# Two modulation weight loads on ScalarE's queue, filler matmuls of 512 columns and a new table of issue in a one-core block of conditioned layer norms, dilated local attention and a token-mixing MLP

## The chip, the core and the metric

The kernel runs on one NeuronCore of a Trainium2 chip. The core has five engines, each with an instruction queue of its own that it works through in order: TensorE (PE in the profile; its weight loads are listed apart as PEld), VectorE (DVE), ScalarE (ACT), GpSimd (POOL) and SyncE (SP), which here only issues DMAs. Sixteen DMA engines move data. The metric is the device time of one execution in microseconds (us); shorter is better.

## What is computed

The input x has 2048 tokens of 512 features. A vector c of 512 numbers gives six modulation vectors; the block normalises, attends and mixes over tokens. Cut to what matters:

```python
mod = (silu(c) @ w_mod).reshape(1, 6, 1, 512)
sa, ca, ga, sb, cb, gb = (mod[:, i] for i in range(6))
h = layernorm(x) * (1 + ca) + sa
x = x + ga * A(h)          # attention
h = layernorm(x) * (1 + cb) + sb
x = x + gb * B(h)          # MLP over tokens

def A(x):                  # 32 heads of 16; 8 keys per query, 2 tokens apart
    q, k, v = split(x @ wqkv)
    idx = pos[:, None] - 2 * arange(8)      # masked where negative
    attn = softmax(q . k[idx] / 4)
    return (attn . v[idx]) @ wo

def B(x):                  # mixes over the 2048 tokens, hidden size 1792
    h = layernorm(x)
    u = gelu(einsum('sd,sf->df', h, w1) + b1)
    return (einsum('df,fs->ds', u, w2) + b2).T
```

All inputs are bfloat16. The parts of w_mod are numbered 0 to 5 in the order sa, ca, ga, sb, cb, gb.

## The kernel before

**Operations and order.** The kernel does not emit instructions where its loops stand. Each step is added to a graph (`add`, `G.add_any`) with a name, the engines it may run on, what it reads and writes and the buffers it takes and frees. `G.schedule` (lines 87 to 114) then walks through `ORDER` (lines 180 to 232), a table of names written out ahead, and every engine gets its instructions in that order. A suffix picks the engine: `:a` ScalarE, `:d` VectorE, `:p` GpSimd, `:s` nothing where the step may be skipped. `:q` on a TensorE step makes `mm` (line 512) issue each matmul as four of 32 output columns; I call these narrow, the others full. Since every engine works in order, an instruction that waits holds up everything behind it in its queue.

**Stages.** The 16 tiles of 128 tokens are worked in five chunks of 2, 4, 4, 4 and 2 tiles.

- *Loads:* `ld_x*` bring x (128 KB a tile; x0 and x1 singly, the others in pairs: `ld_x_1_2` is the pair of tiles 2 and 3 of chunk 1), `ld_wqkv0` to `2` the three parts of wqkv and `ld_wmod0` to `5` the six of w_mod (512 KB each). All are issued by SP through `dma` (line 352); ScalarE issues `ld_c` and later some of the stores.
- *Modulation:* TensorE turns c into columns (`cps`), ScalarE and VectorE make SiLU of it (`silu_exp`, `silu_dve`), and TensorE multiplies it with parts 1 and 0 of w_mod: `modcols1` gives 1 + ca (`a1col`), `modcols0` gives sa (`sab`, from which `qvb0` and `qvb1` make biases of q and v). Parts 2 to 5 give rows (`modrow`, `mrows`, `ld_row*`), one of which scales the output weights (`woq_s`).
- *Filler:* `warm0` is a group of matmuls of the identity with itself, issued behind `cps` while TensorE has nothing to do; `warm1` and up can be placed anywhere or skipped (lines 518 to 528, 533).
- *First norm:* `ln1s*` (statistics, on VectorE, or on ScalarE as two passes with `ln1v*` behind them), `rstd1_*` and `nb1_*`, `n1_*` (the normalised tile). Chunks 0 and 1 are transposed by TensorE (`tr*`) and copied with the scale 1 + ca (`hT*`), chunks 2 to 4 by DMA (`xt*`), and `wsc*` scales the weights for them.
- *Attention of a chunk:* `qkv{chunk}_{t}{j}` are four column groups each of q, k and v (t = 0, 1, 2), copied out by `ev*`. VectorE multiplies q with the eight shifted k (`qk{chunk}_{0..3}`), TensorE adds up over a head (`red*`), then the softmax (`max`, `sub`, `exp`, `esum`, `rcp`, `smB`). SP copies the weights (`a2_*`) and v (`vd*`) to other partitions; VectorE multiplies them (`pv*`), TensorE adds up (`pvacc*`), `oev*` copies out.
- *Output and second norms:* `wo*` is the output projection of a tile. With `x1_*` on ScalarE it has a fifth matmul that adds the residual; with `:d` VectorE adds it. Then `ln2q`, `ln2m`, `n2_*`, the modulation `aff*` of a whole chunk on VectorE, `ln3s`, `nb3_*` and the normalised input `h3_*` of the MLP. `halo_v*` copies the last values of v into the next chunk's buffer.
- *MLP:* `mlp1_{part}_{f}_{tile}` accumulates hidden group f over tokens as far as h3 is there; `park` and `padd` store and add partial sums, `gelu`, then `mlp2_*`, `fin*` and the stores `st_out*`.

**DMA semaphores.** DMAs take turns at eight semaphores, over both queues together, and one that takes a semaphore waits until the DMA that had it before has landed.

All instructions stand in the profile under line 131, the helper that records them, so tiles and operations tell them apart. The lines that the change touches:

Of the kernel before, what the change touches and what calls it, by code (L numbers as in the profile page):

```python
# [185 lines left out]
rstd1_2 nb1_2 n1_7:p ev0_00 ln1s10 n1_9 ln1s11 ev0_10 ld_x_4_14 warm2:s n1_6 qkv1_10 n1_8 qk0_1 qk0_0 qkv0_12 ev0_12  # L186
qk0_2 qk0_3 ln1v11 qkv1_00 ld_wmod4 ln1v10 qkv0_22 ln1v12 qvb1 ld_wmod2 ev1_00 ln1v13 rstd1_3 nb1_3 qkv0_20 qvb_cp1
red0_0 ev1_10 wsc2_3 red0_1 ln1s14:a red0_2 red0_3 mask ld_wo0 xt6 ev0_20 ev0_22 ln1v14 ld_wmod5 vd0_1 qkv1_01 max0
qk1_0 ev1_03 sub0 qkv1_13 wsc1_2:p exp0 ev1_13 qk1_3 xt8 esum0 qkv1_11 halo_v1:a qkv1_02:q ev1_01 rcp0 smB0 ev1_11
wsc0_2:a qkv1_12 qkv1_20 wsc2_2:a wsc0_0:a ev1_02 qk1_1 xt9 xt7 qkv1_22 ev1_12 a2_0_1 wsc1_0:a wsc1_1:a a2_0_2 a2_0_0  # L190
qkv2_00 n1_11:p a2_0_3 ev1_20 qkv1_23:q red1_0 red1_1 qkv1_21:q wsc2_1:a qk1_2 pv0_1 vd0_0 ln1s15:a red1_2 red1_3
ev2_00 pv0_0 ev1_23 vd0_3 n1_10 qkv2_11:q ev1_21 n1_13 max1 pvacc0_0 ln1v15 qkv2_12 vd0_2 pv0_3 ev2_12 ld_wmod3 ld_wo1
qkv2_10 sub1 ev2_10 pvacc0_1 ev1_22 xt10 qkv2_02 exp1 ld_wo3 modrow pv0_2 ev2_02 mrows vd1_2 qkv2_01:q ld_wo2 pvacc0_2
qkv2_13 ev2_11 vd1_3 ld_row0 esum1 qkv2_03 qk2_0 xt11 wsc2_0:a qk2_2 pvacc0_3 ev2_01 vd1_1 qk2_1 qkv2_22:q ev2_13 rcp1
rstd1_4 oev0_2 xt13 ev2_03 oev0_0 smB1 qk2_3 qkv2_20 halo_v2:a woq_s a2_1_2 nb1_4 red2_0 n1_12 red2_1 red2_2 ev2_20
ev2_22 a2_1_3 qkv2_21 red2_3 a2_1_1 qkv2_23:q n1_15 ev2_21 wo0 x1_0 a2_1_0 ev2_23 wo1:q max2 xt12 vd1_0 pv1_2 ln2q0
x1_1 ln2q1 ld_row1 sub2 exp2 qkv3_03:q pvacc1_2 n1_14:p qkv3_22 ld_b2 ev3_22 pv1_3 ln2m0 ev3_03 qkv3_13 vd2_2 esum2
rstd2_0 qkv3_00 qkv3_02 pv1_0 nb2_0 qkv3_01 rcp2 pv1_1 xt14 oev1_2 ev3_00 smB2 vd2_3 ld_row2 n2_1 pvacc1_0 ev3_13
a2_2_2 a2_2_3 n2_0 ev3_01 ev3_02 xt15 qk3_3 qkv3_12:q pvacc1_1 qkv3_10 qkv3_11 oev1_1 ev3_10 oev1_0 pvacc1_3 ev3_12
aff0 qkv3_21 oev1_3 wo2:q a2_2_0 ev3_11 ln3s0:a qk3_0 wo5 wo3 ln3s1:a ln3v0 x1_5 x1_2 halo_v3:a wo4 x1_3 qkv4_00  # L200
a2_2_1 qk3_1 qk3_2 x1_4 ln2q3 red3_0 vd2_1 red3_1 pv2_3 qkv3_20 ln2q2 ln2q5 ev3_21 ln2q4 ld_b1 qkv4_10:q biascols
ev3_20 qkv4_12:q red3_2 ln2m2 rstd2_2 pv2_1 ev4_10 nb2_2 ev4_00 red3_3 pvacc2_3 max3 ev4_12 qkv4_20:q qkv4_22 sub3
qkv4_02:q n2_2 qkv3_23 n2_5 oev2_3 ld_w1_0_0 ln3v1 n2_4 rstd3_0 exp3 pv2_2 pvacc2_2 ld_w1_0_896 ev4_02 vd2_0
ld_w1_0_512 n2_3:p ev3_23 oev2_2 pvacc2_1 pv2_0 nb3_0 oev2_1 aff2 pvacc2_0 esum3:q oev2_0 wo9 rcp3 biascols_cp vd3_2
smB3 ev4_20 vd3_3 wo7 h3_1:p ln3s5 ln3s4 ln3v4 ln3s3:a h3_0:p wo6 wo8 ln3v5 x1_7 x1_9 ln3v3 ln3s2 halo_v4:a x1_6
mlp1_0_0_0 ln3v2 mlp1_0_3_0 rstd3_2 mlp1_0_2_0 qk4_0 x1_8 nb3_2 h3_4:d red4_0 vd3_0 ld_w2_4 h3_5 h3_2:d mlp1_0_8_0
warm1:s warm3:s h3_3 mlp1_0_1_0 ln2q7 mlp1_0_0_2:q a2_3_3 qk4_1 ln2q6 ln2q9 vd3_1 red4_1 a2_3_1 mlp1_0_2_2:q ln2q8
qk4_2 mlp1_0_1_2:q park0_0 park0_1 red4_2 qk4_3 red4_3 a2_3_2 a2_3_0 mlp1_0_3_2 ln2m6 rstd2_6 pv3_1 ld_w1_0_1152 nb2_6
max4 ev4_22 mlp1_0_5_0 park0_2 mlp1_0_4_0 n2_9 mlp1_0_4_2 mlp1_0_6_0 sub4 pv3_0 mlp1_0_5_2 n2_7 n2_6 mlp1_0_8_2 vd4_0
mlp1_0_6_2 pv3_3 park0_3 park0_4 ld_w2_0 pvacc3_0 park0_5 exp4 oev3_0 park0_6 ld_row3 pvacc3_1 mlp1_0_7_0:q pvacc3_3  # L210
mlp1_0_7_2:q pv3_2 esum4:q mlp1_0_10_0:q oev3_1 n2_8 ld_w1_0_1408 rcp4 aff6 pvacc3_2 smB4 oev3_3 mlp1_0_10_2 oev3_2
ln3s6:a a2_4_2 wo12 ln3s9 ln3s7:a ln3v9 x1_12:d wo13 x1_13:d ln2q12 ln3s8 ln3v8 wo11 ln3v7 ln3v6 mlp1_0_12_0
mlp1_0_12_2 wo10 x1_11:d a2_4_0 rstd3_6 nb3_6 a2_4_1 vd4_2 a2_4_3 mlp1_0_9_0 h3_8:d mlp1_0_9_2 x1_10:d ln2q13 h3_9
h3_7:d vd4_1 ln2q10 pv4_2 vd4_3 ln2q11 ln2m10 rstd2_10 mlp1_0_11_0 pv4_3 nb2_10 h3_6:p mlp1_0_7_6 mlp1_0_8_6 pv4_0
mlp1_0_9_6 pv4_1 park0_7 ld_w2_1 park0_8 mlp1_0_11_2 n2_11 n2_12 n2_13 n2_10:d aff10 ln3s13 park0_9 mlp1_0_10_6 ln3v13
pvacc4_2 pvacc4_3 oev4_2 mlp1_0_12_6:q ld_w1_0_1664 ld_w2_2 pvacc4_0 pvacc4_1 oev4_0 mlp1_0_11_6 wo15 x1_15:d
ld_w1_1_0 big_done wo14 x1_14:d ln3s11 mlp1_0_13_0 mlp1_0_13_2 ld_w1_1_640 park0_10 park0_11 park0_12 ln2q15 ln2q14
ln2m14 mlp1_0_13_6 rstd2_14 mlp1_1_1_6 ln3s12 nb2_14 n2_14 mlp1_1_0_6 ln3s10 n2_15:p ln3v12 aff14 mlp1_1_4_6 ln3v11
ln3v10 warm5:s rstd3_10 nb3_10 h3_10 h3_13:p ln3s14 ln3v14 mlp1_1_5_6 ln3s15 ln3v15 mlp1_1_6_6 mlp1_1_0_10 mlp1_1_4_10
h3_12:p park0_13 mlp1_1_2_6 rstd3_14 ld_w1_1_896 mlp1_1_1_10 mlp1_1_6_10 nb3_14:s h3_11 mlp1_1_2_10 padd1_0 h3_14:d  # L220
ld_w2_7 h3_15:d padd1_1 mlp1_1_5_10 mlp1_1_3_6 mlp1_1_3_10 padd1_2 padd1_3 padd1_4 mlp1_1_10_10 padd1_10 mlp1_1_7_10
padd1_7 mlp1_1_8_10 gelu7 gelu10 mlp1_1_9_10 ld_w1_2_0 padd1_5 padd1_6 mlp1_2_0_11 mlp1_2_4_11 mlp1_2_0_14 padd1_9
gelu9 mlp1_2_1_11 ld_w1_1_1408 padd2_0 padd1_8 gelu0 mlp1_2_3_11 mlp1_2_3_14 mlp1_2_1_14 padd2_1 mlp1_2_2_11
ld_w1_2_640 mlp1_2_5_11 mlp1_2_5_14 padd2_3 gelu1 mlp1_2_2_14 padd2_5 gelu5 mlp1_1_11_10 ld_w2_5 padd2_2 gelu3
mlp1_2_4_14 padd2_4 ld_w2_15 padd1_11 gelu2 gelu4 mlp1_2_6_11 mlp1_1_13_10 gelu8 gelu11 ld_w2_9 padd2_6 mlp1_1_12_10
# [798 lines left out]
```

## Time and profile before

| | us |
|---|---|
| median of 3 runs | 202.74 |
| lowest, highest | 201.93, 203.73 |
| the profiled execution | 201.83 |
| its span in the profile | 199.6 |
| granted TensorE clock over it | 1.00 |

The profile is of one execution. PE, PEld, DVE, ACT and POOL are the busy times of the engines; a "q" behind an engine's name is its queue of DMA issues and waits. A line of the order of time gives the start, the length, the engine, the operation, out<-in by tile names and a count; in brackets stands the idle time ahead of it and what ended it. q1 is SP's DMA queue and q10 is ScalarE's. Where I give the start or landing of one step, it is read from the trace by the step's place in its engine's order.

### The profile page before, as it was taken

What the parts mean: (1) busy time and instruction counts of PE and PEld (TensorE: products, weight loads), DVE (VectorE), ACT (ScalarE), POOL (GpSimd) and SP (SyncE); (2) the same over time, 40 slices, a digit from 0 to 9 for tenths busy, and PEclk for the clock granted to TensorE, in tenths of its full rate; (3) what the DMA queues carried; (4) which work ended last, traced back from release to release, by engine and by line L of the source; (5) the groups of instructions that cost most, each with busy time, mean ns of one, the idle gap of its engine ahead of it and who ended that gap; (6) DMA issues with size and microseconds to landing.
All of it is one profiled execution on the core that took longest, in us unless ns stands there. A gap on an engine that the chain in (4) does not pass through costs nothing.

```text
span 199.6 us, 4192 instructions
## 1 busy us (share of the span) xinstructions
PE 189.8 (95%) x1652; PEld 96.2 (48%) x1652; DVE 157.2 (79%) x229; ACT 125.9 (63%) x285; POOL 17.7 (9%) x41
## 2 busy tenths in 40 slices
...
GB/s 152 339 365 319 62 220 174 205 268 189 181 276 50 184 347 132 113 298 168 193 246 20 241 221 200 305 213 243 211 193 168 122 22 155 113 79 26 79 54 55
DMA packets 55367, 35.92 MB, mean 180 GB/s; under 512 B 24628, under 2 KB 52788, under 8 KB 55348
## 3 DMA queue, kind: packets, MB, share of 16 engines
...
q10 hardware_dynamic: 1592, 1.38, 2.1%
...
q14 instruction: 6, 0.05, 0.1%
...
## 4 chain that ended last, share of the span: by engine, by line
PE 40%; DVE 29%; ACT 12%; DMA 8%; SPq 6%; issue 3%; ACTq 0%; DVEq 0%
PE psS L131 39%; DVE big L131 18%; DVE h L131 7%; SPq L131 6%; ACT junk L131 4%; DMA wst<-in_A_wqkv_dram 4%; ACT h L131 3%; DMA out_dram<-h 2%; DMA hT<-h 2%; ACT xx L131 1%; DMA a2sb<-lsb 1%; PE psL L131 1%; DVE st L131 1%; DVE xx L131 1%; DVE m L131 1%
## 5 line engine op out<-in xcount | busy, mean ns | idle before, releaser
L131 PE MATMUL psS<-h,wst 128*128 128x512 bf16 (+1 forms) x296 | 51.2, 379 | 0.4 <-ACT h L131 0.4
L131 PEld LDWEIGHTS <-wst 128*128 128x128 bf16 (+1 forms) x458 | 34.8, 101 | 34.3 <-issue 4.1
L131 DVE TENSOR_TENSOR big<-a2sb,vD 128x4096 bf16<-128x4096 bf16 (+1 forms) x20 | 36.6, 1860 | 1.8 <-PE psL L131 0.8
L131 DVE TENSOR_TENSOR big<-q_sb,k_f 128x4096 bf16<-128x4096 bf16 (+1 forms) x20 | 36.4, 1858 | 0.1
L131 PE MATMUL psS<-hT,w_qkv 128*32 128x256 bf16 (+3 forms) x312 | 30.3, 332 | 1.0 <-DMA hT<-h 1.0
L131 DVE SCALAR_TENSOR_TENSOR h<-psS,bcol,rows_bc 128x512 f32<-128x512 f32 (+2 forms) x18 | 12.4, 690 | 21.0 <-PE psS L131 20.7
L131 PEld LDWEIGHTS <-w_qkv 128*32 128x32 bf16 (+1 forms) x354 | 19.0, 109 | 18.4 <-issue 4.8
L131 PE MATMUL psS<-gT,big 128*128 128x512 bf16 x112 | 24.8, 379 | 0.0
L131 ACT ACTIVATE junk<-xx 128x512 bf16<-128x512 bf16 x28 | 17.6, 627 | 2.6 <-DVE xx L131 1.4
L131 PEld LDWEIGHTS <-big 128*128 128x128 bf16 x144 | 11.9, 97 | 14.9 <-DMA big<-in_w_mod_dram 1.6
L131 ACT ACTIVATE h<-xx,nb,rs 128x512 bf16<-128x512 bf16 x21 | 16.4, 809 | 2.4 <-DVE nb L131 2.3
L131 PE MATMUL psS<-woq,o_sb 128*128 128x512 bf16 (+1 forms) x88 | 16.0, 380 | 0.3 <-ACT o_sb L131 0.3
L131 ACT ACTIVATE gT<-psS,bcol 128x512 bf16<-128x512 f32 x14 | 8.9, 686 | 9.9 <-DVE psS L131 9.9
L131 DVE TENSOR_TENSOR psS<-psS,gT 128x512 f32<-128x512 f32 x14 | 9.2, 696 | 6.3 <-PE psS L131 6.2
L131 DVE TENSOR_TENSOR h<-h,xx 128x512 bf16<-128x512 f32 (+2 forms) x18 | 11.4, 633 | 3.4 <-DMA out_dram<-h 2.7
L131 POOL TENSOR_SCALAR h<-xx,rs,nb 128x512 bf16<-128x512 bf16 x8 | 6.3, 790 | 76.6 <-DVE nb L131 45.5
L131 PEld LDWEIGHTS <-group 128*32 128x32 bf16 x288 | 6.5, 95 | 11.4 <-issue 4.6
L131 PE MATMUL psS<-hT,wst 128*128 128x256 bf16 (+2 forms) x76 | 11.5, 337 | 0.0
L131 ACT ACTIVATE v_sb<-psS,qvb 128x512 bf16<-128x512 f32 (+1 forms) x20 | 11.3, 597 | 0.0
L131 DVE TENSOR_TENSOR h<-h,rows_bc 128x2048 bf16<-128x2048 bf16 (+1 forms) x10 | 10.6, 1055 | 0.8 <-ACT gT L131 0.5
L131 PE MATMUL psS<-big,group 128*32 128x512 bf16 (+1 forms) x160 | 10.0, 339 | 0.8 <-ACT q_sb L131 0.6
L131 ACT ACTIVATE q_sb<-psS,qvb 128x512 bf16<-128x512 f32 (+1 forms) x18 | 10.6, 614 | 0.1
...
## 6 DMA issues: line engine op xcount, KB each, us to landing
...
```

Of the source, the lines that this page charges most:

```text
L131: r = fn(*a, **k)
```

## The change

Three things change. `dma` gets a parameter for the issuing queue, and `ld_wmod1` and `ld_wmod0` are issued by ScalarE. The filler matmuls read the 128 columns of the identity four times over, so each has 512 columns, and their counts are 12 for `warm0` and 2 for the others (64 and 16 of 128 columns before). And the whole table of issue is new; in it only `warm7` and `warm0` are not skipped (`warm0` alone before).

```diff
-    WARM=(64, 16, 16, 16, 16, 16),
+    WARM=(12, 2, 2, 2, 2, 2, 2, 2),
...
-    def dma(out_ap, in_ap, nbytes, reads, writes, name, rate=350e3, issue=0.5, lat=2.0, row=1024, **kw):
-        return add("sp", issue, lambda: nc.sync.dma_start(*(a() if callable(a) else a for a in (out_ap, in_ap))),
+    def dma(out_ap, in_ap, nbytes, reads, writes, name, rate=350e3, issue=0.5, lat=2.0, row=1024, queue="sp", **kw):
+        by = dict(sp=nc.sync, act=nc.scalar, pool=nc.gpsimd)[queue]
+        return add(queue, issue, lambda: by.dma_start(*(a() if callable(a) else a for a in (out_ap, in_ap))),
...
     for v in (1, 0):
         dma(wmodA[:, :, v * D:(v + 1) * D], wmod_view[:, :, v * D:(v + 1) * D], D * D * 2, [], [("wmodA", v)],
-            f"ld_wmod{v}", **(dict(behind=first) if first else dict(alloc=s_wm)))
+            f"ld_wmod{v}", queue="act", **(dict(behind=first) if first else dict(alloc=s_wm)))
...
-                nc.tensor.matmul(ps(s_w)[:, 0:P], lhsT=ident[:], rhs=ident[:], start=True, stop=True)
+                nc.tensor.matmul(ps(s_w), lhsT=ident[:], rhs=_ap(ident[:, 0:1], [[0, 4], [1, P]]), start=True, stop=True)
...
-    add("pe", 5.3, f_warm0, after=[G.ops[-1]], alloc=s_w0, frees=s_w0, writes=["wmA1"], name="warm0")
+    add("pe", 0.216 * WARM[0], f_warm0, after=[G.ops[-1]], alloc=s_w0, frees=s_w0, writes=["wmA1"], name="warm0")
```

The beginning of the table, from which each engine's queue can be read:

```diff
-ld_x1 ident ld_c cps act_table silu_exp silu_dve consts ld_x_2_6 warm0 ln1s7 ld_x_1_4 ln1s1:a warm4:s ln1s5 ld_x0
-ld_x_1_2 ln1v1 ln1s4:a ln1s0 ld_x_2_8 ld_wmod1 ln1v4 ln1v5 ln1s3 ln1v0 rstd1_0 nb1_0 ln1s6:a modcols1 ln1s2 ln1v3
-ln1v2 rstd1_1 nb1_1 ld_wmod0 ld_wqkv0 n1_1:p n1_3:d a1col n1_0:p ld_x_3_12 tr0_0 n1_5:d hT0_1:d n1_2 modcols0 n1_4:p
-tr1_2 ln1v7 hT0_0:d ln1v6 ln1s8:a tr1_0 hT0_2:d wsc0_1:p ld_wqkv1 hT0_3:d qkv0_00 ln1v8 ln1s9 wsc0_3:p sab ln1s12
-hT1_2 ld_x_3_10 qvb0 halo0 qkv0_02 ld_wqkv2 hT1_0 wsc1_3:p hT1_1 hT1_3 qvb_cp0 ln1s13 ln1v9 qkv1_03 qkv0_10 ev0_02:d
...
+ident ld_c ld_x_1_4 act_table ld_wmod1 ld_x0 ld_x1 cps ln1s0 ln1s4:a ln1s1 ld_x_1_2 ln1s3 ln1s2:a warm7 ln1v0 ld_wmod0
+ln1s5 ln1v4 ln1v5 ln1v2 ld_x_3_10 ln1v1 silu_exp rstd1_0 nb1_0:s ld_x_2_6 silu_dve ld_wqkv0 ld_x_2_8 ld_wqkv1 ln1v3
+rstd1_1 nb1_1 n1_2:p n1_0:d ld_x_3_12 ld_wqkv2 n1_1:d n1_5:d warm0 modcols1 a1col wsc0_2:p ld_x_4_14 n1_4 ln1s6 ln1s7
+ln1s10 tr0_0 ld_wmod2 n1_3 halo0 tr1_0 hT0_3 tr1_2 wsc0_1:p modcols0 sab hT0_0 hT0_2 ln1s8 ln1s9 ln1v8 ln1v7 hT0_1
+qkv0_00 hT1_1 qvb0 ln1v6 qvb_cp0 qkv0_02:q hT1_3:d ln1s11:a hT1_0 ln1v9 hT1_2:d qkv0_12:q ln1s13 qkv0_10 ln1v11
+rstd1_2 ev0_02 ev0_12 qk0_3 ev0_00 nb1_2 wsc0_3:p ev0_10 qk0_0 qk0_1 qkv1_10 qkv1_11 n1_6 ev1_11 ln1s14:a ld_wmod3
...
```

By engine, the new table orders the start so:

- SP: `ld_x_1_4 ld_x0 ld_x1 ld_x_1_2 ld_x_3_10 ld_x_2_6 ld_wqkv0 ld_x_2_8 ld_wqkv1 ld_x_3_12 ld_wqkv2 ...` (before: `ld_x1 ld_x_2_6 ld_x_1_4 ld_x0 ld_x_1_2 ld_x_2_8 ld_wmod1 ld_wmod0 ld_wqkv0 ld_x_3_12 ld_wqkv1 ...`). By the semaphores' turns `ld_x_3_12` waits until `ld_wmod1` has landed.
- ScalarE: `ld_c`, the table load, `ld_wmod1 ln1s4 ln1s2 ld_wmod0 silu_exp rstd1_0 rstd1_1 n1_4 n1_3 hT0_3 hT0_0 hT0_2 hT0_1 ...`
- TensorE: `cps warm7 warm0 modcols1 tr0_0 tr1_0 tr1_2 modcols0 qkv0_00 qvb0 qkv0_02 qkv0_12 ...` (before: `cps warm0 modcols1 tr0_0 modcols0 tr1_2 tr1_0 qkv0_00 ...`)

The later parts that the prediction speaks of: `qkv2_00` stands behind `modrow`, `red1_*` and the last groups of chunk 1 (before, ahead of them). `max2` stands behind three of the chunk-1 products `pv1_*`, and `woq_s`, `qk2_1` and `qk2_3` between `smB1` and the first of them. `nb3_0` stands behind `aff2` (before, ahead of it), and GpSimd then does `h3_0`, `halo_v4` and `h3_1` (before `h3_1`, `h3_0`). `x1_13` is on ScalarE. The first output projection behind the last chunk-2 product is `wo7` (`wo9` before), and TensorE's steps from there on are the same ones in another order.

More of the change, by code (lines that the diff above doesn't have):

```diff
@@ L186 @@
[L186 to L225, printed above, removed]
```

53 lines of the change are left out of this document (46 added, 7 removed).

## Prediction

> **What bounds the kernel now.** I read the page first (sections 1, 2, 4), then the stages, then TensorE's waits and its order of time, then the DMA queues, and last the landing times of single loads in the trace.
>
> ```profile
> span 199.6 us, 4192 instructions
> PE 189.8 (95%) x1652; PEld 96.2 (48%) x1652; DVE 157.2 (79%) x229; ACT 125.9 (63%) x285; POOL 17.7 (9%) x41
> ...
> PE 40%; DVE 29%; ACT 12%; DMA 8%; SPq 6%; issue 3%; ACTq 0%; DVEq 0%
> ```
>
> ```profile
> 0.00:12.46 12.46, 8.62 (x122) 8.01 (x122) 7.57 (x27) 9.07 (x24) 4.69 (x25) 1.00 0.84 272
> 12.46:50.00 37.54, 36.35 (x404) 20.27 (x408) 36.33 (x42) 34.31 (x72) 4.52 (x8) 1.00 0.82 215
> 50.00:91.00 41.00, 39.71 (x467) 19.10 (x460) 39.95 (x41) 39.67 (x99) 5.36 (x4) 1.00 0.67 202
> 91.00:128.00 37.00, 36.67 (x328) 16.41 (x328) 34.93 (x62) 30.97 (x74) 2.33 (x3) 1.00 0.73 188
> ```
>
> The stages (start:end, length, busy PE, PEld, DVE, ACT, POOL, clock, DMA share, GB/s) show that after 12.46 us TensorE and VectorE are both full until 128; then TensorE alone. The chain changes engine for that reason: it is VectorE's queue to about 82, TensorE's from there. So I split the span into six terms that add to 199.63: the first qkv matmul starts at 12.46; VectorE's first product (qk0_1) at 17.40, 4.94 later; its queue runs to the end of the last chunk-2 product (pv2_0) at 82.47, which is 65.07, of which 63.0 are the start-to-start times of its instructions and 2.06 waits; TensorE takes the first output projection behind it (wo9) at 83.84, 1.37 later; it ends its last matmul at 196.58, which is 112.74, of which 1.04 waits; 3.05 of store and end remain.
>
> The profiled execution took 201.83 (2.2 around its span); the median of the runs is 202.74, 0.91 more. I make the sum against 201.83 and add the difference to the median.
>
> The start is set by loads:
>
> ```profile
> 2.31 5.87 PE L131 MATMUL psS<-ident 128*128 128x128 bf16 x64
> 9.07 0.55 PE L131 MATMUL psS<-sc,big 128*128 128x1 bf16 x16 [0.89 <-DMA big<-in_w_mod_dram]
> 9.94 0.62 PE L131 MATMUL psS<-ident,h 128*128 128x128 bf16 x8 [0.32 <-POOL h L131]
> 10.94 0.55 PE L131 MATMUL psS<-sc,big 128*128 128x1 bf16 x16 [0.39 <-DMA big<-in_w_mod_dram]
> 11.36 1.05 PE L131 MATMUL psS<-ident,h 128*128 128x128 bf16 x16
> 12.46 1.06 PE L131 MATMUL psS<-hT,wst 128*128 128x256 bf16 x8
> ```
>
> Both modulation products start as their weights land. The loads are served in order at 360 GB/s: wmod1 landed at 9.02 (1.84 MB through), wqkv0 at 12.41 (2.88 MB), wqkv1 at 14.67 (3.67 MB).
>
> **The change, part by part.** *Queue.* ScalarE issues wmod1 behind its table load, which ends at 2.67, so about when SP issues its fifth load (0.8 + 5 x 0.47): early enough. It issues wmod0 only behind two groups of statistics (ln1s4, ln1s2). ln1s2 waits for SP's fourth load; that many bytes (0.79 MB) were through at 6.38, when VectorE's wait for x0 ended; with 1.38 for the group (its two halves in the trace) wmod0 is issued at 7.7. By then SP has issued wqkv1, now its ninth load (before, as the eleventh, its issue ended at 7.35). So wmod0 moves from eighth to eleventh in the line: 3.67 MB lie ahead of its landing. What does a queue of ScalarE get beside a busy SP queue? Two stores of ScalarE ran beside weight loads of SP late in the kernel. One was issued from 167.84 to 168.18; in the next 2 us not one packet of its queue (q10) ran, and it came as q1 emptied:
>
> ```profile
> DMA packets 1233, 0.63 MB, mean 320 GB/s; under 512 B 0, under 2 KB 1233, under 8 KB 1233
> ...
> q1 hardware_dynamic: 1233, 0.63, 107.4%
> ```
>
> ```profile
> q1 hardware_dynamic: 240, 0.11, 38.7%
> q10 hardware_dynamic: 144, 0.13, 37.7%
> ```
>
> (168.18 to 170.15, then 170.2 to 171.2.) The other store landed after 3.8 us in the same way; alone a store takes 1.4 to 1.8. So I take first come, first served: wmod0 lands at 14.67, as the load with 3.67 MB ahead of it did before. modcols0 stands ahead of all qkv matmuls on TensorE and takes 0.42 to the next start: qkv starts at 15.1, **2.65 later**. The other bound is an equal share of 180 GB/s from about 8.3: wmod0 lands at 11.2, and qkv starts at 12.2, now set by the four hT0 copies that moved to ScalarE (four of about 0.36, half of the 0.71 that an ev pair of 256 columns takes, behind n1_3): 0.3 earlier. I keep the first, since two rows show it. SP loses two issues of 0.5, which is worth nothing while six loads stand in line.
>
> [...]
>
> *Filler.* Of the 64 matmuls of 128 columns the first 42 followed at 107 ns and the rest at 56. At 3.33 and 1.69 ns a column, 14 of 512 columns (warm7 and warm0; the others are skipped) take 4.6 us slow and 0.7 fast, 5.3 against 5.87, and end near 7.6. modcols1 waits for wmod1 and for the SiLU behind ScalarE's statistics until about 8.9. So 0; the cover is 1.3.
>
> *Order, VectorE.* First product: 15.1 + 0.87 (qkv0_00) + 0.53 (qvb0) + 0.98 + 0.9 (qkv0_02, qkv0_12) + 0.16 drain + 0.58 (ScalarE's copy ev0_12) = 19.1, against 17.40: **+1.7**. Work from there to the last chunk-2 product: ev0_20 (0.61), ln1s12 (0.82) and nb1_2 (0.07) come in, wsc2_3 (0.26) and three small ones (0.25) go: 64.0 against 63.0, **+1.0**. Waits: two large ones stood there, 0.84 ahead of pv0_1 and 0.67 ahead of pv1_2. Ahead of pv1_1 there are now qk2_1, qk2_3 and woq_s (2 x 2.20 + 1.14 = 5.5) over five SP issues of 0.62 and a landing of 2.0 (5.1); before, it was 4.55. The wait for the chunk-0 copies shrinks too, since xt8, xt7, xt9 and four copies take as long as qk1_2 and qk1_3. I take 1.0 for 2.06, **-1.1**; bounds 0.5 and 2.06.
>
> *Order, TensorE.* A switch between full matmuls and 32-column ones costs about 0.125:
>
> ```profile
> 30.89 1.03 PE L131 MATMUL psS<-hT,w_qkv 128*128 128x512 bf16 x4 [0.97 <-DMA hT<-h]
> 31.85 1.06 PE L131 MATMUL psS<-hT,h 128*32 128x512 bf16 x16
> 32.74 1.03 PE L131 MATMUL psL<-big,group 128*32 128x512 bf16 x16
> 33.61 1.03 PE L131 MATMUL psS<-hT,h 128*32 128x512 bf16 x16
> ```
>
> From start to start four full matmuls take 0.96 ahead of narrow ones (0.863 otherwise), the first narrow group 0.89, the next 0.87. The new table has 34 switches after the start for 44, but eight of the ten saved lie ahead of the output projection of chunk 2, where VectorE sets the time: 0. The two behind it save 0.25, and wo13 gets its residual matmul back because x1_13 goes to ScalarE: +0.22. The wait of 0.97 ahead of qkv2_00 goes (chunk 1's last qkv work and the modulation rows now stand before it), but lies under VectorE's chain too: 0. Of the 1.04 of waits behind wo9 I keep 0.4: **-0.6**. There is one new risk: nb3_0 now stands behind aff2, so GpSimd's h3_0, halo_v4 and h3_1 are ready 2.9 + 1.8 after the last product if GpSimd takes 0.77 as beside statistics, 2.9 + 4.1 if it takes 2.25 and 1.60 as beside large products; TensorE comes 5.7 after. So 0 to +1.3; beside it now stand statistics: 0. Tail: the same stores, 0.
>
> Sum: 1.7 + 1.0 - 1.1 - 0.6 = **+1.0**: 202.8 for an execution like the profiled one, **203.7** as the median. Its own range, with waits at their bounds (-0.5, +1.1) and GpSimd (+1.3) or an empty dip at 2.5 to 5.3 us filled (-0.6): 202.5 to 205.5.
>
> **The rivals.** *The queues share.* Against it the two stores; for it, that those loads moved packets of 256 and 512 bytes, and these move 1,024. First product at about 16.2 instead of 19.1: 2.9 less, 200.8; with all waits gone 200.0.
>
> *TensorE cools (slower).* Between the last tr1 group (about 12.2) and modcols0 it would now stand idle for 2.5; before, the longest idle time was 0.89 and the granted clock stayed at 1.00. If it falls to the slow rate, 4.6 us run at 107 instead of 56 ns as at the start: 2.3 lost ahead of the first product, 206.0. It decides as soon as the slow rate lasts for 1.1 us lost, since 203.7 + 1.1 passes 204.8. No row shows how long an idle time it takes.
>
> [...]
>
> *GpSimd's normalisation becomes the wait* as worked out above: 205.0.
>
> *Nothing comes of the queue:* wmod0 is late, but the other ends meet as before: 202.7, inside the forecast's case.
>
> **How the numbers follow.** First come, first served 0.56, sharing 0.24, cooling 0.13, GpSimd 0.07. About 1% (2.03) is what a measurement of this kernel can tell from no change. Faster than 200.7: over half of sharing, 0.14, and 0.01 else. Slower than 204.8: cooling, most of GpSimd (0.05) and a quarter of the forecast's case: 0.32. Within: 0.53. The range 200.5 to 206.1 leaves out the ends of sharing and of cooling.
>
> **What would show it.** wmod0's landing at 14.0 to 14.7, a wait of over 2 us ahead of modcols0 ended by DMA big<-in_w_mod, the first qkv matmul near 15.1; the first product near 19; no wait ahead of qkv2_00; VectorE's waits for a2sb under 0.3; TensorE from the chunk-2 projection to its end in about 112.1. A first qkv matmul before 13 means that the queues share and the forecast is too slow; 256-column matmuls at over 200 ns behind it mean cooling; a wait on POOL h of over 0.5 near 88 means GpSimd.

## The result and the profile after

| | before | after |
|---|---|---|
| runs | 4 | 4 |
| median (lowest to highest), us | 202.94 (201.93 to 203.73) | 208.59 (207.55 to 209.63) |
| profiled execution, its span | 201.83, 199.6 | 208.26, 206.0 |
| granted clock over the span | 1.00 | 0.974 |

After against before is 1.0295, 95% interval 1.0242 to 1.0348: slower, and above the range of the prediction. The kernel before has one more run here than in the three given ahead of the prediction (202.74). Intervals leave out runs more than 1.5% above the fastest of the same kernel; medians keep them.

The page of the changed kernel:

```profile
span 206.0 us, 4329 instructions
PE 191.7 (93%) x1726; PEld 96.4 (47%) x1726; DVE 157.2 (76%) x227; ACT 124.0 (60%) x282; POOL 25.9 (13%) x42
...
PEclk9955999999999999999999999999999999999999
...
PE 53%; DVE 23%; DMA 11%; SPq 6%; issue 5%; ACT 1%; DVEq 0%; ACTq 0%
```

VectorE is busy for exactly as long as before (157.2), and TensorE for 1.9 more. The new thing is the line of the clock: slices 3 and 4 (10.3 to 20.6 us) stand at half. Split at the seams of the prediction's six terms (start:end, length, busy PE, PEld, DVE, ACT, POOL, clock, DMA share, GB/s):

```profile
0.00:16.54 16.54, 9.76 (x71) 5.42 (x72) 7.71 (x24) 10.69 (x26) 6.31 (x19) 0.83 0.95 305
16.54:22.67 6.13, 6.13 (x102) 4.80 (x100) 3.54 (x12) 2.06 (x6) 1.22 (x13) 0.62 0.38 120
22.67:88.92 66.25, 62.81 (x790) 32.82 (x787) 64.09 (x54) 61.06 (x136) 13.25 (x5) 1.00 0.70 192
88.92:203.00 114.08, 112.95 (x772) 53.40 (x772) 81.17 (x137) 50.23 (x116) 5.16 (x6) 1.00 0.56 150
```

| term | before | predicted | after |
|---|---|---|---|
| first qkv matmul | 12.46 | 15.1 | 16.54 |
| first product of VectorE | 17.40 | 19.1 | 22.67 |
| VectorE to the end of chunk 2's products | 65.07 | 65.0 | 66.25 |
| output projection behind it | 1.37 | 1.37 | 1.19 |
| TensorE from there to its end | 112.74 | 112.1 | 112.91 |
| tail | 3.05 | 3.05 | 3.02 |

Of the 6.4 us that the span gained, 5.3 stand ahead of the first product. TensorE's order of time shows two places:

```profile
2.33 5.75 PE L131 MATMUL psS<-ident 128*128 128x512 bf16 x14
10.19 0.54 PE L131 MATMUL psS<-sc,big 128*128 128x1 bf16 x16 [2.11 <-DVE sc L131]
10.80 3.01 PE L131 MATMUL psS<-ident,h 128*128 128x128 bf16 x24
16.09 0.58 PE L131 MATMUL psS<-sc,big 128*128 128x1 bf16 x16 [2.29 <-DMA big<-in_w_mod_dram]
16.54 1.88 PE L131 MATMUL psS<-hT,wst 128*128 128x256 bf16 x8
```

TensorE idles 2.1 us ahead of modcols1 and 2.3 us ahead of modcols0. The eight qkv matmuls behind that start 208 ns apart where they started 110 ns apart before (1.88 long for 1.06): the second place costs the wait for wmod0, and the rate goes with the clock (0.50 there, 1.00 before).

In the trace, wmod1 was issued at 1.44, ahead of x1 and x_1_2, and landed at 6.47; x_1_2 then landed at 7.62, so the statistics that wait for it (ln1s2) started at 7.71, and wmod0, behind them, was issued from 8.47 to 8.88 and landed at 16.05. ScalarE's own order shows both issues:

```profile
1.41 1.28 ACT L131 ACT_TABLE_LOAD   x1 [1.41 <-PEq L1009]
1.44 0.42 ACTq L131 DMA_DIRECT2D big<-in_w_mod_dram  x1
...
7.71 0.63 ACT L131 ACTIVATE junk<-xx 128x512 bf16<-128x512 bf16 x1 [2.67 <-DMA xx<-in_A_x_dram]
...
8.46 0.63 ACT L131 ACTIVATE junk<-xx 128x512 bf16<-128x512 bf16 x1
8.47 0.41 ACTq L131 DMA_DIRECT2D big<-in_w_mod_dram  x1
```

Neither issue waited for the end of the instruction ahead of it: the first ran beside the table load (1.41 to 2.69), the second beside the second pass of ln1s2.

### The profile page after: what moved, and what is told of

Same layout as the page of the kernel before. It is cut to its first block, busy times and chain, and to the rows that moved or that the text cites. A ratio compares the mean times of both kernels' runs of the same rounds, so it can differ in the third digit from the quotient of the medians.

```text
span 206.0 us, 4329 instructions
## 1 busy us (share of the span) xinstructions
PE 191.7 (93%) x1726; PEld 96.4 (47%) x1726; DVE 157.2 (76%) x227; ACT 124.0 (60%) x282; POOL 25.9 (13%) x42
## 4 chain that ended last, share of the span: by engine, by line
PE 53%; DVE 23%; DMA 11%; SPq 6%; issue 5%; ACT 1%; DVEq 0%; ACTq 0%
PE psS L131 51%; DVE big L131 15%; SPq L131 6%; DVE h L131 4%; DMA big<-in_w_mod_dram 4%; DMA a2sb<-lsb 3%; DMA xx<-in_A_x_dram 3%; PE psL L131 1%; DMA hT<-h 1%; DVE lsb L131 1%; DVE m L131 1%; ACT v_sb L131 1%; DVE st L131 1%; DVE mv L131 1%; ACT junk L131 0%
## 5 line engine op out<-in xcount | busy, mean ns | idle before, releaser
L131 PEld LDWEIGHTS <-wst 128*128 128x128 bf16 (+1 forms) x554 | 36.3, 104 | 33.1 <-issue 1.7
L131 PE MATMUL psS<-hT,w_qkv 128*32 128x512 bf16 (+3 forms) x336 | 29.3, 343 | 0.6 <-DMA hT<-h 0.5
L131 DVE SCALAR_TENSOR_TENSOR h<-psS,bcol,rows_bc 128x512 f32<-128x512 f32 (+2 forms) x18 | 12.4, 690 | 22.8 <-PE psS L131 22.5
L131 POOL TENSOR_SCALAR h<-xx,rs,nb 128x512 bf16<-128x512 bf16 x6 | 14.3, 2380 | 62.2 <-DVE nb L131 37.6
L131 ACT ACTIVATE junk<-xx 128x512 bf16<-128x512 bf16 x26 | 16.4, 629 | 4.0 <-DMA xx<-in_A_x_dram 3.5
L131 ACT ACTIVATE h<-xx,nb,rs 128x512 bf16<-128x512 bf16 x19 | 15.0, 814 | 2.2 <-DVE nb L131 2.0
L131 PE MATMUL psS<-hT,wst 128*32 128x256 bf16 (+3 forms) x124 | 13.7, 372 | 0.0
L131 ACT ACTIVATE q_sb<-psS,qvb 128x512 bf16<-128x512 f32 (+1 forms) x20 | 11.4, 599 | 2.6 <-PE psS L131 2.5
L131 DVE BATCH_NORM_STATS2 st<-xx 128x6 f32<-128x512 bf16 x11 | 7.4, 674 | 6.0 <-DMA xx<-in_A_x_dram 6.0
L131 ACT ACTIVATE o_sb<-psS 128x512 bf16<-128x512 f32 x16 | 9.1, 594 | 2.9 <-PE psS L131 2.7
```

The lines of the kernel that those rows point to most:

```text
L131: r = fn(*a, **k)
```

## The experiments

My theory from the two traces was that two things cost the time, the late landing of wmod0 and the halved clock, and that the new table by itself costs little. The rivals were that the table is what costs, and that the clock costs nothing because loads set the first product. The medians below the second row are to be read beside the kernel before on the same chip (202.39 to 202.78). The times of single steps are those of one profiled execution each.

| kernel | median | ratio, interval | mean clock of its runs | modcols0 | first qkv | first product |
|---|---|---|---|---|---|---|
| before (profiled) | 202.94 | | 1.00 | 10.94 | 12.46 | 17.40 |
| changed | 208.59 | 1.0295, 1.0242 to 1.0348 | 0.974 or 0.975 | 16.09 | 16.54 | 22.67 |
| both loads on SyncE | 204.78 | 1.0068, 1.0019 to 1.0117 | 0.975 to 1.00 | 13.68 | 14.16 | 20.83 |
| wmod0 early | 205.36 | 1.0126, 1.0052 to 1.0199 | 0.975 to 0.992 | 14.28 | 14.74 | 18.92 |
| more filler | 205.05 | 1.0122, 1.0056 to 1.0189 | 0.992 to 1.00 | 15.78 | 16.19 | 20.37 |
| before, 14 wide | 204.03 | 1.0059, 1.0013 to 1.0105 | 0.982 to 0.992 | 11.02 | 13.12 | 18.28 |
| SyncE and filler | 202.18 | 0.9954, 0.9916 to 0.9993 | 1.00 in 10 of 11 | 12.42 | 12.82 | 17.25 |
| wmod0 midway, filler | 202.55 | 0.9979, 0.9942 to 1.0017 | 1.00 in 10 of 11 | 13.03 | 13.44 | 17.88 |
| before, 18 wide | 203.79 | 1.0054, 1.0015 to 1.0093 | 1.00 in 8 of 11 | 11.69 | 13.21 | 18.16 |
| before, 78 narrow | 201.74 | 0.9944, 0.9908 to 0.9979 | 1.00 in 9 of 11 | 10.83 | 12.33 | 17.56 |
| before, queue used first | 203.54 | 1.0049, 1.0016 to 1.0082 | 0.99 in 9 of 11 | 12.74 | 14.88 | 20.35 |
| before, queue alone | 210.92 | 1.0418, 1.0370 to 1.0465 | 0.966 to 0.975 | 18.33 | 20.44 | 27.00 |
| norm on ScalarE | 202.37 | 1.0009, 0.9974 to 1.0045 | 1.00 in 9 of 11 | 12.67 | 13.08 | 17.51 |
| changed, narrow filler | 208.12 | 1.0257, 1.0207 to 1.0307 | 0.983 or 0.984 | 17.11 | 17.55 | 24.23 |

### Both loads on SyncE again

```diff
-            f"ld_wmod{v}", queue="act", **(dict(behind=first) if first else dict(alloc=s_wm)))
+            f"ld_wmod{v}", **(dict(behind=first) if first else dict(alloc=s_wm)))
```

> The changed kernel with the two loads (wmod1, wmod0) issued by SyncE again, at the same places of the new table; filler and table stay. My reading of the 6.4 us that the span gained (206.0 against 199.6): 4.1 because wmod0 lands at 16.05, about 1.2 to 1.9 because the clock fell at 10.96, 1.1 in VectorE's wait for the chunk-0 weight copies, near nothing else. By it wmod0 becomes the sixth load of SyncE, with 1.8 MB through at its landing, so it lands before 10, there is no wait ahead of modcols0, and the first qkv matmul follows the transposes at 13.0 to 13.9. The clock still falls at about 11, since the idle time between filler and modcols1 is unchanged, but comes back before 18 because TensorE no longer stands still. First product 18.2 to 20, span 201.5 to 203.5, time 204 to 206. Rival, the new order itself is what costs (VectorE's and GpSimd's queues): the start mends, and the time is given back later: over 206.5. Rival, the queue is the only cost: 202 to 203.

wmod0 landed at 8.64 and nothing waited for it, as expected, and the median (204.78) is in the range given. The first qkv matmul (14.16) came 0.26 and the first product (20.83) 0.83 later than that range: the clock fell at 10.01 and came back only at 20.25 in the profiled execution. That execution has three halved windows like the changed kernel's, so the two compare: a span of 204.05 against 206.04. Most other runs lost fewer (clock 0.991 to 1.00 in six of ten).

### wmod0 issued directly behind wmod1

```diff
-ident ld_c ld_x_1_4 act_table ld_wmod1 ld_x0 ld_x1 cps ln1s0 ln1s4:a ln1s1 ld_x_1_2 ln1s3 ln1s2:a warm7 ln1v0 ld_wmod0
+ident ld_c ld_x_1_4 act_table ld_wmod1 ld_wmod0 ld_x0 ld_x1 cps ln1s0 ln1s4:a ln1s1 ld_x_1_2 ln1s3 ln1s2:a warm7 ln1v0
```

> The changed kernel with wmod0 issued by ScalarE directly behind wmod1 (at about 1.9) instead of behind two groups of statistics. First come, first served (a load starts when those issued before it have been served, on whichever queue): wmod0 lands at 7.0 to 8.0, and x1, x_1_2 and all behind them land about 1.4 later than in the changed kernel (x1 8.3, x_1_2 9.1), so the statistics, SiLU and modcols1 come 1.4 later (11.6), and the first qkv matmul at 14 to 15.3. Equal sharing of the bandwidth between the queues: x1 and x_1_2 lose at most 0.7, wmod0 lands at 8.5 to 9.5, and the first qkv matmul stands at 13.0 to 14. Time by the first 204.5 to 207, by the second 203.5 to 205.5. If the place of issue behind the statistics were not what made wmod0 late, it would land after 13 still.

wmod0 landed at 7.71, so it was the place of issue that made it late. x_1_2 came at 8.36 (0.74 later) and x1 at 5.96 (0.94 earlier): between the two rules. modcols1 moved from 10.19 to 10.86 and the clock fell for one window at 11.16. The first qkv matmul came 1.80 earlier (14.74).

### More filler

```diff
-    WARM=(12, 2, 2, 2, 2, 2, 2, 2),
+    WARM=(21, 2, 2, 2, 2, 2, 14, 2),
...
-ln1s10 tr0_0 ld_wmod2 n1_3 halo0 tr1_0 hT0_3 tr1_2 wsc0_1:p modcols0 sab hT0_0 hT0_2 ln1s8 ln1s9 ln1v8 ln1v7 hT0_1
+ln1s10 tr0_0 ld_wmod2 n1_3 halo0 tr1_0 hT0_3 tr1_2 warm6 wsc0_1:p modcols0 sab hT0_0 hT0_2 ln1s8 ln1s9 ln1v8 ln1v7 hT0_1
```

(`warm6` stood further down the table before, skipped.)

> The changed kernel with more filler and nothing else: warm0 has 21 matmuls for 12, which fills the 2.1 us ahead of modcols1, and a group of 14 stands between the last transposes and modcols0, which fills the 2.3 us there. If the fallen clock is a cost of its own: the granted clock stays full from about 7.5 on, wmod0 lands at 16.0 as before, the first qkv matmul stays at 16.5, its 256-column groups run at about 110 ns for 208, and the first product comes at 20.5 to 21.2 for 22.67; time 206.0 to 207.3 for 208.6. If the clock costs nothing because loads and copies set the first product: it stays at 22.3 to 22.8 and the time at 208.2 to 209.

```profile
2.41 7.59 PE L131 MATMUL psS<-ident 128*128 128x512 bf16 x23
9.84 0.54 PE L131 MATMUL psS<-sc,big 128*128 128x1 bf16 x16
10.41 1.03 PE L131 MATMUL psS<-ident,h 128*128 128x128 bf16 x9
11.64 1.01 PE L131 MATMUL psS<-ident,h 128*128 128x128 bf16 x15 [0.20 <-ACT h L131]
12.49 3.19 PE L131 MATMUL psS<-ident 128*128 128x512 bf16 x14
15.78 0.55 PE L131 MATMUL psS<-sc,big 128*128 128x1 bf16 x16
16.19 1.04 PE L131 MATMUL psS<-hT,wst 128*128 128x256 bf16 x8
```

The clock held (1.00 from 7.42 to 17.65). wmod0 was nearly as late as before (15.73 for 16.05), but the qkv group takes 1.04 for 1.88 and the first product comes 2.30 earlier; the span is 202.79 for 206.04. The clock is a cost of its own. The median, 205.05, is below the 206.0 to 207.3 expected: 0.95 of the gain stands behind the first product, in TensorE's last term (111.95 for 112.91), where the clock is 1.00 in both kernels.

### The kernel before with 14 wide filler matmuls

```diff
-    WARM=(64, 16, 16, 16, 16, 16),
+    WARM=(14, 2, 2, 2, 2, 2),
...
-                nc.tensor.matmul(ps(s_w)[:, 0:P], lhsT=ident[:], rhs=ident[:], start=True, stop=True)
+                nc.tensor.matmul(ps(s_w), lhsT=ident[:], rhs=_ap(ident[:, 0:1], [[0, 4], [1, P]]), start=True, stop=True)
```

> The kernel before with one part of the change alone: 14 filler matmuls of 512 columns for 64 of 128. If the filler is worth nothing, as predicted: it ends within 0.3 of where it did (8.18), the clock stays full, the first qkv matmul stays at 12.3 to 12.7, and the time within 0.5% of the kernel before. Rival, wide fillers warm or keep the clock differently (fewer weight loads, another busy share): the granted clock falls somewhere ahead of 14, and the time is 0.5 to 2 us longer.

The rival held. The filler ended at 7.70 for 8.18, modcols1 started at 9.61 (wmod1 landed at 9.56 for 9.02), and no run kept the clock for its whole length. What I had priced at nothing costs 1.6 us in the median (1.2 by the ratio). Not all of that is shown to be the clock's: of the 2.34 by which this span (201.97) is longer, 0.88 stands ahead of the first product, and 1.49 is VectorE's term (66.56 for 65.07), where the two waits for copied weights are 1.56 and 1.53 for 0.84 and 0.67.

### Both costs taken away, and two other fillers

Both loads on SyncE as above, and:

```diff
-    WARM=(12, 2, 2, 2, 2, 2, 2, 2),
+    WARM=(23, 2, 2, 2, 2, 2, 2, 2),
```

> The changed kernel with both loads on SyncE again and warm0 at 23 matmuls for 12, so that TensorE stands idle neither ahead of modcols1 nor ahead of modcols0. If late wmod0 and the fallen clock are the whole cost of the change, and the new table by itself is worth nothing: the clock stays full, the first qkv matmul starts at 12.9 to 13.3 (behind the transposes), the first product at 17.1 to 17.6 (4.2 later, as with full clock in the run with more filler), then 66.2, 1.2, 112.0 and 3.0 as there: span 199.5 to 200.3, time 201.7 to 202.5, within 0.5% of the kernel before. If the table's later part has a price of its own that the late start hid: 203.3 or more.

First product 17.25, span 199.98, time 202.18: inside what was expected, and the first qkv matmul (12.82) 0.08 ahead of it. With the two costs gone the new table is as good as the old one, within 0.4 us of the old one with its clock kept (201.8 in the median, below).

With wmod0 kept on ScalarE, between its two groups of statistics:

```diff
-    WARM=(12, 2, 2, 2, 2, 2, 2, 2),
+    WARM=(21, 2, 2, 2, 2, 2, 2, 2),
...
-ident ld_c ld_x_1_4 act_table ld_wmod1 ld_x0 ld_x1 cps ln1s0 ln1s4:a ln1s1 ld_x_1_2 ln1s3 ln1s2:a warm7 ln1v0 ld_wmod0
+ident ld_c ld_x_1_4 act_table ld_wmod1 ld_x0 ld_x1 cps ln1s0 ln1s4:a ld_wmod0 ln1s1 ld_x_1_2 ln1s3 ln1s2:a warm7 ln1v0
```

> The changed kernel with wmod0 kept on ScalarE, but issued between its two groups of statistics (at about 5.0 for 8.5), and warm0 at 21. A load of ScalarE's queue has landed at 7.71 when issued at 1.88, at 15.73 when issued at 8.09, at 16.05 when issued at 8.47. If it begins only when what SyncE had issued until then is through (first come, first served): 2.6 to 2.8 MB stand ahead of its landing, it starts moving at about 9 to 10 and lands at 10.8 to 12.3. If it shares with SyncE's queue from its issue on: half of 360 GB/s from about 7, landing 9.5 to 10.2. By both it is in time for the transposes: first qkv matmul 12.9 to 13.5, span 199.5 to 200.6, time 201.7 to 202.8. Rival, a second cost of ScalarE's queue beside the late landing (its statistics later by the issue): over 203.5.

The time is as expected, the landing is by neither rule: 12.93, issued from 4.29 to 4.67.

The kernel before with 18 wide matmuls, which differs from the one with 14 by

```diff
-    WARM=(14, 2, 2, 2, 2, 2),
+    WARM=(18, 2, 2, 2, 2, 2),
```

> The kernel before with 18 filler matmuls of 512 columns. With 14 the filler ended at 7.70 for 8.18, modcols1 came 1.9 later and the clock was halved from 10.19 to 13.60. If the idle time decides: the filler now ends at 8.4 to 8.6, the idle time is again under 1.2, the clock stays full in at least half of the runs, time 201.3 to 202.7. If the width decides (fewer matmuls and weight loads in the same time count as less work): the clock falls in nearly every run all the same, first qkv matmul at 13 and time 203.2 to 204.5.

The clock stayed full (0.999 or 1.00) in 8 of 11 runs, so width alone did not lose it here. But the time was missed (203.79 for at most 202.7): wmod1 landed at 10.29 (9.02 before), and VectorE's term is 65.97 for 65.07. Why the loads came later is open.

The kernel before with more of its own narrow filler:

```diff
-    WARM=(64, 16, 16, 16, 16, 16),
+    WARM=(78, 16, 16, 16, 16, 16),
```

> The kernel before with 78 filler matmuls of 128 columns for 64. The filler ends at 8.9 to 9.1 for 8.18, just ahead of modcols1. The kernel before has runs with a mean clock of 0.998 to 1.000 (201.2 to 202.3) and runs with 0.99 (202.4 to 204.1), one halved window in the latter. If that window comes of the idle time behind the filler: all runs now at 0.997 or more, and a median of 201.2 to 202.0. If it comes from elsewhere: a mixture as before and 202.2 to 202.7. If the filler pushes modcols1 back: up to 0.3 more.

201.74: faster than both kernels, for 14 more matmuls that nobody reads. Two of the eleven runs still lost a window (0.989 and 0.990), where none was expected. Beside all experiments together, the kernel before has 36 runs at a mean clock of 0.997 or more with a median of 201.8, and 43 at about 0.99 with 203.0: a halved window goes with 1.2 us.

### The queue in the old table

The kernel before with 78 narrow matmuls, and both loads on ScalarE directly behind its table load (`dma` gets its parameter as in the change, and the two names leave their old places further down):

```diff
-ld_x1 ident ld_c cps act_table silu_exp silu_dve consts ld_x_2_6 warm0 ln1s7 ld_x_1_4 ln1s1:a warm4:s ln1s5 ld_x0
+ld_x1 ident ld_c cps act_table ld_wmod1 ld_wmod0 silu_exp silu_dve consts ld_x_2_6 warm0 ln1s7 ld_x_1_4 ln1s1:a warm4:s ln1s5 ld_x0
```

> The kernel before with its own table and 78 filler matmuls of 128 columns (201.74 by itself), and with both modulation loads issued by ScalarE directly behind ld_c (at 1.4 and 1.9): the queue used as early as it can be. By the rule read so far (a load of ScalarE's queue shares half and half with SyncE's once it moves, and moves early when little stands ahead): wmod1 lands at 5.7 to 6.2 for 9.4, wmod0 at 7.6 to 8.1 for about 10.8, and x_1_2 and x_2_8 land 1.0 to 1.5 later (8.0 and 9.3). The products wait for nothing then, but the statistics of chunk 1 do: first qkv matmul 12.3 to 13.2 for 12.33; time 201.6 to 202.8. If loads and not statistics set the start: first qkv matmul at 11.3 to 11.9, time 200.5 to 201.2.

```profile
2.32 6.17 PE L131 MATMUL psS<-ident 128*128 128x128 bf16 x78
8.32 0.54 PE L131 MATMUL psS<-sc,big 128*128 128x1 bf16 x16
12.23 0.72 PE L131 MATMUL psS<-ident,h 128*128 128x128 bf16 x8 [3.37 <-POOL h L131]
```

Missed on the slow side: wmod0 landed at 8.96, but x0 only at 8.64 and x_1_2 at 9.40 (6.73 with the loads on SyncE), the transposes waited 3.37 for the normalised tile, and the clock fell at 12.62 for one window. The queue brings little bandwidth (286 GB/s over the first 12 us, for 273 with the same filler and the loads on SyncE); most of what it takes, the loads of x lose.

The kernel before with the queue alone changed, its table and filler as they are (`dma` gets its parameter as in the change):

```diff
-            f"ld_wmod{v}", **(dict(behind=first) if first else dict(alloc=s_wm)))
+            f"ld_wmod{v}", queue="act", **(dict(behind=first) if first else dict(alloc=s_wm)))
```

> The kernel before with the queue alone changed: both modulation loads issued by ScalarE at the places that its own table gives them, wmod1 behind two groups of statistics (6.4 to 6.8), wmod0 behind a third (about 9.7). Three loads of ScalarE's queue began to move 3.5 to 3.6 after the end of their issue while SyncE's queue was full, and then got half of the packets. By this rule wmod1 begins at 10.3 and lands at 13.0 to 14.0, wmod0 lands at 15.8 to 17.2; TensorE stands idle from 8.2, the clock is halved from about 10.2 for two or three windows, the first qkv matmul comes at 16.3 to 17.7, time 207.5 to 210. If a load begins only when all that was issued before it has landed: wmod1 by 6.8 has at least 2.3 MB ahead and lands by 10.5 to 11.5, since SyncE has issued fewer bytes by then; time 204.5 to 206. If ScalarE's queue costs nothing by itself: 202 to 203.

```profile
14.34 0.59 PE L131 MATMUL psS<-sc,big 128*128 128x1 bf16 x16 [5.94 <-DMA big<-in_w_mod_dram]
14.79 1.01 PE L131 MATMUL psS<-ident,h 128*128 128x128 bf16 x8
18.33 0.59 PE L131 MATMUL psS<-sc,big 128*128 128x1 bf16 x16 [2.53 <-DMA big<-in_w_mod_dram]
```

Both products, and so the loads that they wait for, come some 0.3 and 1.1 later than the late end of what was expected by the rule (wmod0 was issued at 10.61, not 9.7), the first qkv matmul 2.7 later (20.44), the median 0.9 (210.92), and four windows are halved in the profiled execution. This one edit costs 8 us in the old table; the new table had at least moved wmod1 to the front.

### One normalisation off GpSimd, and the narrow filler

On top of "SyncE and filler", at the same place in the table:

```diff
-red1_0 n1_13:p a2_0_1 qkv1_20:q red1_1 a2_0_2 warm3:s red1_2 qk1_3 vd0_0 ev1_21 mrows ev1_22 red1_3 pv0_1 ev1_20
+red1_0 n1_13:a a2_0_1 qkv1_20:q red1_1 a2_0_2 warm3:s red1_2 qk1_3 vd0_0 ev1_21 mrows ev1_22 red1_3 pv0_1 ev1_20
```

> The changed table with both loads on SyncE and the longer filler (202.18), and one normalisation (n1_13) on ScalarE for GpSimd. In all seven executions with the new table it took GpSimd 5.28 beside VectorE's large products, and the last chunk-0 weight copies landed within 1.0 of its end (34.62 and 34.80 beside an end of 34.51; 35.10 and 35.25 beside 35.14); in the kernel before, without GpSimd there, each copy lands 0.65 behind the one before it. If GpSimd's work is what holds the copies: the four land 0.65 apart, the last at about 1.4 behind the end of its issue, VectorE's wait for a2sb ahead of pv0 falls from 1.16 to under 0.3, and the time falls by 0.5 to 1.0, to 201.2 to 201.7. If the copies are late for another reason (transposes and v copies in the same queue): the wait stays at 0.8 to 1.3 and the time at 202.0 to 202.6; ScalarE's extra 0.8 can add up to 0.3.

The theory fell: the last copy landed at 35.17, 1.85 behind the third, and VectorE still waited 1.26. The profile puts this wait, and the 1.15 of "SyncE and filler", down to TensorE's sums (PE psL), which ended at 35.19 and 34.94, just behind the last copies (35.17 and 34.80); the two are too close to tell which VectorE waited for.

The changed kernel with its filler as 8 and 56 matmuls of 128 columns:

```diff
-    WARM=(12, 2, 2, 2, 2, 2, 2, 2),
+    WARM=(56, 2, 2, 2, 2, 2, 2, 8),
...
-                nc.tensor.matmul(ps(s_w), lhsT=ident[:], rhs=_ap(ident[:, 0:1], [[0, 4], [1, P]]), start=True, stop=True)
+                nc.tensor.matmul(ps(s_w)[:, 0:P], lhsT=ident[:], rhs=ident[:], start=True, stop=True)
```

> The changed kernel with the filler alone undone: 64 matmuls of 128 columns (8 and 56) for 14 of 512. In the kernel before, wide filler alone cost 1.6 in the median (204.03 for 202.39), with the clock halved in all ten runs for half of them. If what counts in the changed kernel is that TensorE stands idle for 2.1 ahead of modcols1, however wide the matmuls ahead of it are: the filler ends at 8.0 to 8.4, the idle time is 1.8 to 2.2, the clock still falls at 10.5 to 11.5 for two or three windows, wmod0 lands at 15.7 to 16.3, time 207.6 to 208.9 for 208.59. If the width is a cost of its own (the clock, or slower loads beside it): the clock keeps or falls for one window only, and the time is 205 to 207.

```profile
2.46 5.67 PE L131 MATMUL psS<-ident 128*128 128x128 bf16 x64
9.74 0.54 PE L131 MATMUL psS<-sc,big 128*128 128x1 bf16 x16 [1.61 <-DVE sc L131]
...
17.11 0.59 PE L131 MATMUL psS<-sc,big 128*128 128x1 bf16 x16 [4.53 <-DMA big<-in_w_mod_dram]
17.55 1.88 PE L131 MATMUL psS<-hT,wst 128*128 128x256 bf16 x8
```

The time is as expected, the way is not: the clock outlived the first idle time (1.61), and fell at 16.77 by the second (4.53). The width alone is not what the changed kernel pays for. That the times nearly agree is luck: wmod0 landed at 17.06 and the first product came at 24.23, 1.56 later than in the changed kernel, while VectorE's and TensorE's later terms are 0.99 and 0.94 shorter (65.26 and 111.97).

## Why the prediction was wrong, and where it was right

Four spans make a square; three windows are halved in the left column, none in the right one:

| new table | clock halved | clock kept |
|---|---|---|
| wmod0 late | 206.04 | 202.79 |
| wmod0 early | 204.05 | 199.98 |

So by the span of one execution each the clock costs 3.3 to 4.1, the late load 2.0 to 2.8, and 0.35 is left over the 199.63 of before. At the first product, which the two act on directly, it is 2.3 to 3.6 (20.37 and 17.25 for 22.67 and 20.83) and 1.8 to 3.1; up to 0.95 of the span's difference comes later, at full clock, and is not shown to be the clock's.

Two steps of the prediction failed: the landing of wmod0, put at 14.67, and the filler, priced at 0. Either one alone leaves the median inside the predicted 200.5 to 206.1 (205.05 with the clock kept, 204.78 with the load early); together they took it to 208.59. By the prediction's steps, with 206.04 - 200.63 = 5.41 to explain:

*The start (first qkv matmul predicted at 15.1, measured at 16.54: 1.4 too early).* The direction and the mechanism, a wait ahead of modcols0 ended by the load, were right. The step that failed here is "ScalarE issues wmod1 behind its table load, which ends at 2.67": it was issued at 1.44, beside the table load. The bytes ahead of x_1_2 were then 0.5 MB more than I counted, ln1s2 started at 7.71 instead of about 6.4, and wmod0 was issued at 8.47 instead of 7.7, behind x_3_12 and wqkv2 too (0.76 behind the start of ln1s2 and not the 1.38 of the whole group, which hid 0.6 of the delay). I had read one rule (who is issued first is served first) off two stores and not followed its first consequence inside the same queue change. From the end of its issue to its landing wmod0 took 7.2; issued from 7.7 it would by that have landed at about 15.3 (an estimate), so some 0.8 of the 1.4 is the late issue and 0.6 how the queue was served.

*First come, first served against sharing.* Each holds for a part. From the end of its issue (8.88) to 12.4, one packet of wmod0 moved; from 13 to 15 each queue moved about half of the packets:

```profile
DMA packets 1247, 1.22 MB, mean 348 GB/s; under 512 B 57, under 2 KB 1247, under 8 KB 1247
q1 hardware_dynamic: 1246, 1.22, 110.2%
q10 hardware_dynamic: 1, 0.00, 0.1%
```

```profile
q10 hardware_dynamic: 384, 0.39, 55.5%
q1 hardware_dynamic: 381, 0.38, 53.4%
```

(8.9 to 12.4, and 13 to 15.) In the kernel with wmod0 midway the issue ended at 4.67 and the packets began at 7.9; in "queue alone" at 6.40 and 10.0. So there was a delay of 3.2 to 3.6 behind a full queue of SyncE, and then about half of the packets (273 of 567 from 9.5 to 11 with wmod0 midway, 195 of 386 from 11.5 to 12.5 in "queue alone", 384 of 765 in the changed kernel), although in the last x_3_12 and wqkv2 had been issued earlier. What makes the delay stays open. With only the delay in view (the two stores' 2 us without a packet) I dismissed sharing too far; the delay and the half rate together made the landing later than both of my numbers (14.67 and 11.2).

*Filler, priced at 0 with a cover of 1.3.* Wrong. The cover was time in which nothing waits, but in these traces the clock went with how busy TensorE was in windows of 3.41 us (it was half from 10.96 to 21.20, three of them). In the kernel before, the window from 6.79 was busy for 2.20; in the changed kernel the one from 7.54 for 1.24, and the clock was half from its end on:

```profile
7.54:10.96 3.42, 1.24 (x20) 0.68 (x18) 3.13 (x14) 2.90 (x10) 0.44 (x1) 1.00 1.10 357
10.96:14.37 3.41, 2.76 (x24) 2.29 (x23) 3.09 (x9) 3.29 (x8) 3.10 (x7) 0.50 1.09 362
14.37:17.78 3.41, 1.69 (x22) 1.31 (x23) 1.03 (x4) 1.76 (x5) 3.03 (x18) 0.50 1.10 365
17.78:21.20 3.42, 3.42 (x67) 2.67 (x69) 2.51 (x8) 0.91 (x4) 0.22 (x1) 0.50 0.29 90
```

*TensorE cools: a rival at 0.13, and the clock did fall (0.50 from 10.96 to 21.20).* That it cools is a name of mine: the traces show the granted clock, not what lowers it. Its price was near, in part by luck: 2.3 ahead of the first product predicted, 22.67 - 20.37 = 2.30 measured, but 0.35 of that is that wmod0 landed 0.32 earlier in the execution with more filler; from the first qkv matmul to the first product the clock costs 6.13 - 4.18 = 1.95. Its place was not right: I looked at the idle time ahead of modcols0, and the clock had fallen before that by the one ahead of modcols1 (2.11; the SiLU waits for ln1s2, which waits for x_1_2, so by the order of the landings it is the early wmod1 again; no run moves wmod1 alone). And the idle time that my chance for it assumed is shown by no row. Between the changes of the clock lay 3.41 us or a multiple of it (10.19 to 13.60 with 14 wide matmuls, 10.01 to 20.25 with both loads on SyncE), and of the seven windows at whose end it fell ahead of 17 us, six had TensorE busy for 0.39 to 1.51. The profiled executions kept the clock with 1.67 busy or more in a window and lost it with 1.51 or less:

```profile
6.79:10.20 3.41, 2.20 (x45) 1.94 (x44) 2.64 (x11) 2.49 (x9) 1.71 (x3) 1.00 1.05 351
194.28:197.69 3.41, 1.67 (x29) 1.49 (x27) 2.19 (x7) 0.00 (x0) 0.00 (x0) 1.00 0.26 76
6.77:10.19 3.42, 1.51 (x24) 0.78 (x23) 2.40 (x10) 2.78 (x9) 2.00 (x3) 1.00 0.96 331
```

(Before, kept; 78 narrow, near its end, kept for one window more; 14 wide in the old table, halved from 10.19.) The longest idle stretch inside a window sorts the same windows as well: kept with 1.75 or less, lost with 1.91 or more. No run tells the two apart.

*VectorE (65.0 predicted, 66.25).* The work was right: 64.0 predicted, 64.09 busy. The waits were not: 1.0 for 2.06 predicted, 2.2 measured. The one ahead of chunk 1's weights went, as worked out; the one ahead of pv0_1 grew from 0.84 to 1.88:

```profile
DVE big L131 <- DMA a2sb<-lsb: 1.9, 1, 1.9
DVE big L131 <- ACT k_f L131: 1.8, 1, 1.8
```

I had counted issues ahead of the copies; those were done in time (the first copy was issued at 34.81, when the weights were ready at 34.79), but the last of the four landed at 40.85, 2.6 behind the one before it. In seven of the eight profiled executions of the new table one of the four lands 1.6 to 2.6 behind the one before it; in the eighth (the narrow filler) they land 0.65 apart, VectorE does not wait, and the term is 65.26, near the predicted 65.0. The old table shows it too, with 14 wide filler matmuls (2.0): a late copy stands in eight of the nine executions with wide filler and in none of the five with narrow. Nothing shows how a filler that ends over 20 us earlier could act on the copies. Taking GpSimd's work away from beside them did not mend it; what holds the copies stays open. The second line is the first product's wait and belongs to the start.

*TensorE to the end (112.1 predicted).* 112.91 in the changed kernel, with two waits, for ScalarE (0.59) and VectorE (0.48), and 111.95 with more filler, with one of them; the clock is 1.00 there in both. No wait stood ahead of qkv2_00, and GpSimd's normalisation made none, as forecast. Tail: 3.02, right.

Together: 1.45 (load) + 2.1 (from there to the first product, 1.95 of it the clock) + 1.25 (VectorE) - 0.2 (projection) + 0.8 (TensorE) - 0.03 = 5.4.

*Slips in the working.* The loads were not all served at 360 GB/s: by the landings that I gave, 1.04 MB took 3.39 us (about 310) and the next 0.79 MB 2.26 (350). 107 and 56 ns for 128 columns are 0.84 and 0.44 ns a column, not 3.33 and 1.69; the sum of 5.3 us comes out with these. The filler took 5.75 and ended at 8.08 instead of 7.6, because the clock rose at 7.54 in this execution and at 6.79 in the one before (with both loads on SyncE it rose at 6.60, and the same filler ended at 7.61). And 203.7 with both late terms (1.1 and 1.3) is 206.1, not the 205.5 given for the forecast's own case.
